# Attention with a routed mixture of experts: new places for the routing of the next-to-final batch, and two output copies on another engine

## The chip, the cores and the metric

The kernel runs on one core of a Trainium2 chip. A core has five engines that run side by side and wait for one another through semaphores: TensorE (PE, the matrix engine; PEld is its weight load), VectorE (DVE), ScalarE (ACT), GpSimd (POOL) and SyncE (SP), which here only starts transfers. The metric is the device time of one execution in microseconds (us). The kernel before takes 797.64 us, the median of three runs (795.63 to 798.19).

## The reference

There are two halves. The first is causal attention for 8 batches of 8 heads, 576 rows each, head size 64, with a bias from a running sum:

```
bias   = -(cum[:, :, :, None] - cum[:, :, None, :])
scores = where(causal, -1e9, q @ k.T / 8 + minimum(bias, 0))
attn   = softmax(scores);  x = attn @ v
```

The second takes the 4608 rows of `x` (512 wide) through one of 8 experts each:

```
logits = x @ w_gate;  e = argmax(logits);  gate = softmax(logits)[e]
out    = gate * (maximum(x @ w1[e], 0) @ w2[e])
```

## The kernel before, in words

**Attention.** Heads go in 32 pairs, four pairs to a batch of 576 rows. The class Attention walks a loop of turns; in turn n each engine gets what the table `ORDER` lists, item by item, each with an offset that says which pair the item is for (pair = n - offset). The order in which the program issues these items is the order of the instructions on PE, DVE, ACT and POOL, since the loop runs under a manual schedule. Items that matter here, for turn n:

- `S0` to `S4`: the score products of five row groups on PE, each into a buffer `s`, of which there are two, used in rotation (pool `ps_s`, PSUM); `R..`: masked row maximum on DVE, which frees that buffer; `X..`: exponential on ACT.
- `T0` to `T4`: transposes of the exponentials on PE into a buffer `t` (two of these as well, pool `ps_t`); `E0` and `E4` copy the result to `aT` on DVE, `E1` to `E3` on ACT (line 325 and 324, the function `copy`).
- `AV`: attention times v on PE (line 335), 36 matmul records for one pair, for the pair of the turn before; it too takes a buffer `t`. `XB`: its output goes to `xb` by the function `keep`, on DVE, one turn later still.

Turn 31 is the last with scores; turn 32 has the rest of pair 31, up to its AV.

**Routing.** When the four pairs of a batch are in `xb`, the batch is routed in eight steps, the generator `route`. Its first part issues PE work into an `s` buffer; after the `yield` comes the work of another engine that empties it. Step 0: logits (PE, line 378), then the copy `LT` on ACT. Step 1: transposes of `LT` (PE), then `part` on DVE, after which the generator lives on as `self.chain`, in three more pieces: sums to `dd` (DVE, four instructions, lines 400 to 409), `ex` (ACT, line 411), one-hot and gate (DVE, six small instructions, lines 413 to 423). Step 2: ranks by counting (PE), then the row numbers `dsi` (DVE, lines 439 to 445). Steps 3 to 7: transpose one fifth of the rows (PE), then scale it into `xr` (DVE, line 455). When `dsi` is there, each finished fifth of `xr` can be scattered to its expert's region of the DRAM tensor `xs` by an indirect transfer that POOL starts (line 464).

Batches 0 to 5 are routed in slots of the table: `rp` issues the PE part, `rv` or `ra` the other engine's part some items later. Batch 6, the next-to-final one, is routed in turns 29 to 32 by the list `HASTE`: at each `rp` item the function `hurry` issues whole steps, both parts of a step one straight behind the other, and a -1 or -2 stands for two pieces of the chain. Its scatters are issued at the items `SC` and `SD` and after the loop. Batch 7 is routed after the loop, between the matmuls of expert 0.

**Experts.** After the loop come, in program order, the load of the first 512 rows of expert 0 (`load_x`, line 657), which waits for every scatter issued so far, that is batches 0 to 6; the conversion of the first half of w1 into two rounded parts (`load_w`: ACT high part, line 648, POOL low part, line 649); transposes of the loaded rows (`trans_groups`, line 694), their split (ACT and DVE, lines 626 and 627), and layer 1 of expert 0 (line 722). Weight blocks (`raw`, 1 MB) have two buffers; the third load can go when POOL has converted the first. From there on an expert follows an expert.

The names `p0` to `p7` and `v0` to `v7` in the change are the PE part and the other engine's part of the steps 0 to 7, and `c` is one piece of the chain.

Of the kernel before, what the change touches and what calls it, by code (L numbers as in the profile page):

```python
# [20 lines left out]
B, H, S, D = 8, 8, 576, 64  # L21
# [19 lines left out]
RUNP = NPAIR  # L41
# [1 line left out]
SPLITS = {"QH": 0, "QL": 1, "KH": 2, "KL": 3, "QD": 4}  # L43
EVAC = {0: "V", 1: "A", 2: "A", 3: "A", 4: "V"}
STEPS = (3, 0), (1, 4), (5, 6), (2, 7)
HASTE = [0], [3, 1], [4, -1], [-2, 5], [2, 6], [7], [], []
NROUTE = 8
W_STEP = 2
THIN_AT = (2, 2)
# [23 lines left out]
class Attention:  # L73
# [97 lines left out]
    def load(self, p):  # L171
        x = self.ldx.tile([P, 2 * S], F32, name="qk")
        self.nc.sync.dma_start(x, self.qkv[p][:, : 2 * S])
        self.st.setdefault(p, {}).update(x=x)
# [166 lines left out]

    def keep(self, p):
        b, x = divmod(p, 4)
        self.copy("V", self.xb[b % 2][:, x, :S], self.st.pop(p)["O"])

    def fresh(self, b):
        nc = self.nc
# [128 lines left out]
    def loop(self):  # L476
        self.load(2)
        self.load_v(1)
        self.rows, self.sq, self.chain, self.slot = {}, [], None, {}
        self.haste, self.nrow = list(HASTE), {}  # L480
        self.todo = constants(self.nc, self.const, self.K, self.wg)
        for n in range(-3, RUNP + 3):
            for name, off in ORDER:
                if 0 <= n - off < RUNP:
                    self.item(name, n - off)
        while self.sq:
            self.scatter(*self.sq.pop(0))
        assert self.nfill > E
        self.open = False

    def item(self, name, p):
        kind, arg = name.rstrip("0123456789"), [int(x) for x in name if x.isdigit()]
        if kind == "S":
            if p < 2 and arg[0] == ORD[0]:
                self.load(p + 3)
                if p == 0:
                    self.load_v(2)
                    self.table(3)
            self.scores(p, arg[0])
            if p == 1:  # L500
                next(self.todo, None)
        elif kind == "R":
            self.rowmax(p, *arg)
            self.nrow[p] = self.nrow.get(p, 0) + 1
            if self.nrow[p] == 2 * NG - 1:
                for load, n in (self.table, 4), (self.load_v, 3), (self.load, 5):
                    if p + n < RUNP:
                        load(p + n)
        elif kind == "DM":
            self.causal(p)  # L510
        elif kind == "X":
            self.expo(p, *arg)
            if name == "X11" and 2 <= p and self.nfill <= E:
                for _ in range(2):
                    if self.nfill <= E:
                        self.fill(self.nfill)
                        self.nfill += 1
        elif kind == "T":
            self.st[p]["E", arg[0]] = self.trans(p, arg[0])
        elif kind == "E":  # L520
            self.st[p].pop(("E", arg[0]))()
        elif kind == "AV":
            self.av(p)
        elif kind == "XB":
            self.keep(p)
        elif kind in SPLITS:
            if p:
                self.split(p, SPLITS[kind])
        elif kind in ("SC", "SD"):
            if self.sq and (p >= RUNP - 4 or p % 4 < 2 + (kind == "SC")):  # L530
                self.scatter(*self.sq.pop(0))
        elif p >= 4 or kind in ("ch", "ca"):
            self.routing(kind, p, *arg)

    def routing(self, kind, p, k=0):
        b, x = p // 4 - 1, p % 4
        if kind == "ch" and x == 3:
            self.fresh(p // 4)
        if b == RUNP // 4 - 2:
            if kind == "rp":  # L540
                self.hurry(self.rows[b], self.haste.pop(0))
            elif kind == "ch" and x == 0 and "rr" not in self.rows[b]:
                self.scale(self.rows[b])
        elif kind == "rp":
            self.begin(p, k, self.rows[b], STEPS[x][k])
        elif kind in ("rv", "ra"):
            if (p, k) in self.slot and (kind == "ra") == (self.slot[p, k][1] == 0):
                self.end(p, k)
        elif kind == "ch" and x == 0 and b >= 0:
            self.scale(self.rows[b])  # L550
        elif self.chain and (x == 2 or kind == "ch" and x == 3):
            next(self.chain, None)

    def hurry(self, r, steps):
        if "rr" not in r:
            self.scale(r)
        for x in steps:
            if x < 0:
                for _ in range(2):
                    next(self.chain, None)  # L560
            else:
                self.begin(RUNP, 0, r, x)
                self.end(RUNP, 0)

    def begin(self, p, k, r, x):
        todo = self.route(r, x)
# [448 lines left out]
```

## Time and profile before

| what | value |
|---|---|
| median of three runs | 797.64 us |
| the profiled execution | 792.23 us |
| its span | 790.5 us |
| PE busy | 754.3 us, 95% of the span |
| DVE busy | 453.3 us, 57% |
| ACT busy | 416.8 us, 53% |
| POOL busy | 252.1 us, 32% |

The profiled execution is one run, 5.4 us under the median of the others; 1.7 us of it lies around the span. Sums of trace durations are made against its 792.23 us. PE is busy nearly throughout, so what counts is where PE waits. The page's slices show one dip of the clock that PE was granted in the middle of the span, in the slice from 316 to 336 us: it is the passage from attention to the experts.

### The profile page before, as it was taken

What the parts mean: (1) busy time and instruction counts of PE and PEld (TensorE: products, weight loads), DVE (VectorE), ACT (ScalarE), POOL (GpSimd) and SP (SyncE); (2) the same over time, 40 slices, a digit from 0 to 9 for tenths busy, and PEclk for the clock granted to TensorE, in tenths of its full rate; (3) what the DMA queues carried; (4) which work ended last, traced back from release to release, by engine and by line L of the source; (5) the groups of instructions that cost most, each with busy time, mean ns of one, the idle gap of its engine ahead of it and who ended that gap; (6) DMA issues with size and microseconds to landing.
All of it is one profiled execution on the core that took longest, in us unless ns stands there. A gap on an engine that the chain in (4) does not pass through costs nothing.

```text
span 790.5 us, 17552 instructions
## 1 busy us (share of the span) xinstructions
PE 754.3 (95%) x6664; PEld 583.3 (74%) x6664; DVE 453.3 (57%) x1234; ACT 416.8 (53%) x1001; POOL 252.1 (32%) x362
## 2 busy tenths in 40 slices
PE   7899999999999986799899999999999999999995
PEld 4667777777777764478788887888888887888874
DVE  5777988888898976454163453632632452633420
ACT  4998989999898975423152332412522341513410
POOL 5565677676767662221001001010000001010001
PEclk9999999999999999799999999999999999999998
DMA  7999776777767342459253452620530261720101
GB/s 256 323 320 290 221 249 204 229 226 218 239 220 232 125 152 88 162 178 335 87 196 129 162 174 83 203 89 29 189 134 27 92 231 46 240 95 21 53 29 40
DMA packets 57344, 130.80 MB, mean 165 GB/s; under 512 B 5455, under 2 KB 5455, under 8 KB 57232
## 3 DMA queue, kind: packets, MB, share of 16 engines
q1 hardware_dynamic: 48768, 105.53, 42.0%
q0 software_dynamic: 5936, 18.92, 6.3%
q10 hardware_dynamic: 2528, 4.89, 1.9%
q8 instruction: 67, 1.10, 0.6%
q14 instruction: 45, 0.37, 0.1%
HBM read 101.30 MB, written 28.27 MB: 164 GB/s over the span
## 4 chain that ended last, share of the span: by engine, by line
issue 38%; PE 7%; DMA 6%; another core or an unknown queue 4%; POOL 2%; POOLq 1%; ACT 0%; DVE 0%
DMA out_dram<-y,xr 6%; PE ph L722 3%; PE py L744 3%; POOL out_dram L751 2%; PE t L335 1%; PE t L694 0%; POOLq L844 0%; PE t L302 0%; PE t L378 0%; POOLq L751 0%; POOLq L1010 0%; ACT xT L626 0%; DVE y L750 0%; PE t L702 0%
## 5 line engine op out<-in xcount | busy, mean ns | idle before, releaser
L744 PE MATMUL py<-w2t,hT 128*128 128x512 f32 x768 | 181.4, 392 | 1.0 <-DVEq L858 1.0
L298 ACT ACTIVATE E<-z,m 128x512 f32<-128x512 f32 (+4 forms) x288 | 166.7, 583 | 28.4 <-DVE m L284 21.4
L722 PE MATMUL ph<-xT,w1t 128*128 128x512 f32 x768 | 178.2, 391 | 1.7 <-ACT xT L626 1.2
L722 PEld LDWEIGHTS ph<-xT,w1t 128*128 128x128 f32 x768 | 143.6, 188 | 33.6 <-issue 2.5
L744 PEld LDWEIGHTS py<-w2t,hT 128*128 128x128 f32 x768 | 142.5, 188 | 31.3 <-issue 1.4
L751 POOL DMA_INDIRECT out_dram<-y,xr x39 | 38.1, 977 | 397.3 <-DVE y L750 332.2
L284 DVE CUSTOM_DVE_ANT_0 z<-s,B 128x512 f32<-128x512 f32 (+3 forms) x224 | 116.0, 543 | 15.3 <-PE s L226 7.1
L335 PE MATMUL t<-aT,v 128*64 128x64 f32 (+4 forms) x1152 | 96.3, 322 | 1.3 <-ACT w1t L648 1.0
L226 PE MATMUL s<-kh,q 64*128 64x128 f32 (+3 forms) x512 | 93.1, 372 | 2.5 <-DVE m L284 1.3
L724 ACT ACTIVATE hT<-ph 128x512 fp32r<-128x512 f32 x64 | 38.2, 598 | 102.1 <-PE ph L722 97.1
L750 DVE TENSOR_SCALAR y<-py,xr 128x512 f32<-128x512 f32 x35 | 26.3, 750 | 114.5 <-PE py L744 114.5
L725 DVE SCALAR_TENSOR_TENSOR hT<-ph,hT 128x512 fp32r<-128x512 f32 x64 | 44.1, 690 | 67.4 <-ACT hT L724 63.8
L302 PE MATMUL t<-ident,E 64*128 64x64 f32 x1600 | 75.7, 227 | 6.9 <-ACT aT L325 3.1
L302 PEld LDWEIGHTS t<-ident,E 64*128 64x128 f32 x1600 | 63.8, 139 | 22.1 <-issue 9.6
L325 ACT COPY aT<-t 128x1024 f32<-128x1024 f32 (+2 forms) x96 | 73.1, 795 | 10.0 <-PE t L302 5.1
L226 PEld LDWEIGHTS s<-kh,q 64*128 64x128 f32 x512 | 52.1, 187 | 29.9 <-DVE aT L324 23.5
L335 PEld LDWEIGHTS t<-aT,v 128*64 128x64 f32 x1152 | 51.5, 139 | 22.2 <-issue 11.6
L298 ACT ACTIVATION_READ_ACCUMULATOR E<-z,m 128x1 f32 x288 | 55.4, 192 | 0.0
L464 POOL DMA_INDIRECT xs<-xr,dsi x40 | 40.1, 1001 | 41.5 <-DVE num L966 18.7
L626 ACT ACTIVATE xT<-t 128x512 fp32r<-128x512 f32 x32 | 17.6, 597 | 66.9 <-PE t L694 58.8
L207 POOL TENSOR_TENSOR kl<-qk,kh 128x576 fp32r<-128x576 f32 x30 | 42.6, 1422 | 29.4 <-ACT kh L203 29.4
L324 DVE COPY aT<-t 128x256 f32<-128x256 f32 x64 | 39.6, 619 | 12.6 <-PE t L302 8.6
(157 smaller groups left out, 970.7 us busy)
## 6 DMA issues: line engine op xcount, KB each, us to landing
raw<-in_w_dram SPq DMA_DIRECT2D x32, 1024.0 KB
qk<-in_qkv_dram SPq DMA_DIRECT2D x32, 576.0 KB
B<-cum SPq DMA_DIRECT2D x31, 512.0 KB
v<-in_qkv_dram SPq DMA_DIRECT2D x32, 320.0 KB
B<-cum SPq DMA_DIRECT2D x62, 144.0 KB
xr<-xs SPq DMA_DIRECT2D x8, 1028.0 KB
xs<-blank ACTq DMA_DIRECT2D x9, 514.0 KB
xs<-blank SPq DMA_DIRECT2D x8, 514.0 KB
```

The costliest lines, as they stand in the source:

```text
L207: e.tensor_tensor(out=d["kl"], in0=k, in1=d["kh"].bitcast(F32), op=ALU.subtract)
L226: self.nc.tensor.matmul(out, terms[n][0], terms[n][1], start=begin and n == 0, stop=n == len(terms) - 1, skip_group_check=True)
L284: ins = nc.vector.tensor_tensor_reduce(out=cut(z[:, :w]), in0=x, in1=mask, scale=-0.125, scalar=3.0e38, op0=ALU.add, op1=ALU.min, accum_out=m,
L298: nc.scalar.activation(out, z[:, :w], AF.Exp, bias=m, scale=-1.0, accum_out=total)
L302: self.nc.tensor.transpose(out, src[r], self.K["ident"][r, r])
L325: return self.nc.scalar.copy(o, i)
L335: nc.tensor.matmul(ps[64 * h : 64 * h + 64, bank, lo - 512 * bank : hi - 512 * bank], v[:, kt, h], self.aT[p % 2][:, kt, h, lo:hi], start= ...
L464: ins = self.nc.gpsimd.indirect_dma_start(out=self.K["xs"], out_offset=IndirectOffsetOnAxis(ap=r["dsi"][:n, k : k + 1], axis=0), in_=r["xr ...
L722: nc.tensor.matmul(ps, w[:, a, d, c], x[:, b, d], start=n == 0, stop=n == 11)
L725: nc.vector.scalar_tensor_tensor(out=h[:, 1, f], in0=ps, scalar=0.0, in1=h[:, 0, f].bitcast(F32), op0=ALU.max, op1=ALU.subtract)
L744: self.nc.tensor.matmul(ps, hT[:, a, f, c], w[:, b, f % 4], start=f == 0 and i == 0, stop=f == 7 and i == 2)
L751: disjoint(self.tc, "out", self.nc.gpsimd.indirect_dma_start(out=self.out, out_offset=IndirectOffsetOnAxis(ap=row[:, DM + 1 : DM + 2].bitc ...
```

## The change

The list `HASTE` becomes a table: behind the item on the left, of the pair after the colon, stands the part on the right. Each part of each step of batch 6 has a place of its own, so the PE part and the part that empties its buffer are no longer issued one straight behind the other. All steps stand in turns 29 to 31; before, the last one stood in turn 32. In `hurry`, as soon as `dsi` exists, every fifth that is ready is scattered at once. And `keep` copies the outputs of pairs 30 and 31 on ACT.

```diff
-HASTE = [0], [3, 1], [4, -1], [-2, 5], [2, 6], [7], [], []
+HASTE = {
+    "T4:28": "p0", "ra1:27": "v0", "rp0:28": "p1", "rv0:28": "v1", "ch:29": "c", "SC:29": "c",
+    "XB:28": "c", "rp1:28": "p3", "rv1:28": "v3", "rp0:29": "p2", "rv0:29": "v2", "E0:30": "p4",
+    "XB:29": "v4", "rp1:29": "p5", "rv1:29": "v5", "rp0:30": "p6", "rv0:30": "v6", "T1:31": "p7", "ch:31": "v7",
+}
...
-        self.copy("V", self.xb[b % 2][:, x, :S], self.st.pop(p)["O"])
+        self.copy("V" if p < RUNP - 2 else "A", self.xb[b % 2][:, x, :S], self.st.pop(p)["O"])
...
+        for x in HASTE.get(f"{name}:{p}", "").split():
+            self.hurry(self.rows[RUNP // 4 - 2], x)
...
-            if kind == "rp":
-                self.hurry(self.rows[b], self.haste.pop(0))
-            elif kind == "ch" and x == 0 and "rr" not in self.rows[b]:
+            if kind == "ch" and x == 0:
                 self.scale(self.rows[b])
...
-    def hurry(self, r, steps):
-        if "rr" not in r:
-            self.scale(r)
-        for x in steps:
-            if x < 0:
-                for _ in range(2):
-                    next(self.chain, None)
-            else:
-                self.begin(RUNP, 0, r, x)
-                self.end(RUNP, 0)
+    def hurry(self, r, x):
+        if x[0] == "c":
+            next(self.chain, None)
+        elif x[0] == "p":
+            self.begin(RUNP, int(x[1]), r, int(x[1]))
+        else:
+            self.end(RUNP, int(x[1]))
+            while r["b"] == RUNP // 4 - 2 and "dsi" in r and self.sq:
+                self.scatter(*self.sq.pop(0))
```

How it moves instructions, in three places. The first is ACT in turn 30 of the kernel before, from the last exponential of `E_104` for its second row group to the copies `E3` and `E1` of pair 30; `ex` is the chain's piece of batch 6.

```order
L298 ACTIVATE E_102,sums_208<-z,m 128x128
L298 ACTIVATE E_104,sums_208<-z,m 128x384
L411 ACTIVATE ex<-dd 128x40
L325 COPY aT_107<-t 128x2x8x64
L325 COPY aT_107<-t 128x2x4x64
L298 ACTIVATE E_104,sums_208<-z,m 128x384
```

In the changed kernel `ex` stands a turn earlier, in turn 29, behind the two copies of pair 29 (to the other `aT`) and behind the second `E_104`; the piece begins with the copy `LT` of step 0:

```order
L329 COPY LT<-s 128x576
L329 COPY aT_107<-t 128x2x6x64
L302 ACTIVATE E_102,sums_208<-z,m 128x128
L302 ACTIVATE E_104,sums_208<-z,m 128x384
L329 COPY aT_108<-t 128x2x8x64
L329 COPY aT_108<-t 128x2x4x64
L302 ACTIVATE E_104,sums_208<-z,m 128x384
L415 ACTIVATE ex<-dd 128x40
```

So nothing but exponentials stands ahead of the two copies in turn 30 now.

The second place is the end of attention on ACT in the kernel before: the copy `E2` of pair 31, then the first half of w1 and the split of expert 0's rows.

```order
L298 ACTIVATE E_106,sumx_209<-z,m 128x576
L325 COPY aT_108<-t 128x2x6x64
L648 ACTIVATE w1t<-raw 128x512 x4
L626 ACTIVATE xT<-t 128x8x64 x4
L626 ACTIVATE w1t<-raw 128x512 x4
```

And in the changed kernel, with the two output copies (`xb`, pairs 30 and 31):

```order
L302 ACTIVATE E_106,sumx_209<-z,m 128x576
L329 COPY xb_206<-t 128x576
L329 COPY aT_108<-t 128x2x6x64
L329 COPY xb_206<-t 128x576
L651 ACTIVATE w1t<-raw 128x512 x4
L629 ACTIVATE xT<-t 128x8x64 x4
L629 ACTIVATE w1t<-raw 128x512 x4
```

The second copy, which needs the AV of pair 31, stands ahead of the w1 conversion and of the split.

The third place is POOL from the last bias table to the w1 conversion, in the kernel before: two scatters of batch 5, row numbers for batch 7, five scatters of batch 6.

```order
L169 TENSOR_TENSOR B<-B,mixed 128x64
L464 DMA xs<-xr,dsi 38912x514 x2
L350 IOTA xr 128x5
L464 DMA xs<-xr,dsi 38912x514 x5
L649 TENSOR_TENSOR w1t<-raw,w1t 128x512 x4
```

In the changed kernel four of the five have moved ahead of the row numbers:

```order
L173 TENSOR_TENSOR B<-B,mixed 128x64
L468 DMA xs<-xr,dsi 38912x514 x6
L354 IOTA xr 128x5
L468 DMA xs<-xr,dsi 38912x514
L652 TENSOR_TENSOR w1t<-raw,w1t 128x512 x4
```

Each scatter follows the DVE part that fills its rows, and these are in turns 30 and 31 now.

## Rows read from the trace of the kernel before

**Rows 1.** Timeline: start, duration, engine, line, operation, count, [idle before <- releaser]; AV by pair.

```profile
267.28 2.96 PE L335 MATMUL t<-aT,v 128*64 128x64 f32 x36
276.06 2.96 PE L335 MATMUL t<-aT,v 128*64 128x64 f32 x36
286.79 2.96 PE L335 MATMUL t<-aT,v 128*64 128x64 f32 x36
299.67 2.96 PE L335 MATMUL t<-aT,v 128*64 128x64 f32 x36
309.57 2.96 PE L335 MATMUL t<-aT,v 128*64 128x64 f32 x36 [0.36 <-ACT aT L325]
317.34 4.62 PE L335 MATMUL t<-aT,v 128*64 128x64 f32 x36 [0.97 <-ACT w1t L648]
```

**Rows 2.** Timeline of turn 30, where PE, DVE and ACT wait for one another.

```profile
291.28 0.53 PE L302 MATMUL s<-ident,LT 64*128 64x64 f32 x10 [0.79 <-DVE xr L455]
...
291.85 0.55 DVE L392 TENSOR_TENSOR part<-s,ra 128x160 f32<-128x160 f32 x2 [0.63 <-PE s L302]
...
297.81 0.24 ACT L411 ACTIVATE ex<-dd 128x40 f32<-128x40 f32 x1 [2.27 <-DVE dd L409]
297.95 1.48 ACT L325 COPY aT<-t 128x1024 f32<-128x1024 f32 x2
...
299.00 0.34 PE L302 MATMUL t<-ident,E 64*128 64x64 f32 x4 [1.95 <-ACT aT L325]
```

**Rows 3.** Timeline of turn 31, the same view.

```profile
302.68 0.76 DVE L324 COPY xb<-t 128x576 f32<-128x576 f32 x1 [1.06 <-PE t L335]
...
305.17 0.44 PE L226 MATMUL s<-kh,q 64*128 64x384 f32 x2 [1.06 <-DVE xr L455]
...
307.81 1.71 ACT L325 COPY aT<-t 128x1024 f32<-128x1024 f32 x2 [0.21 <-PE t L302]
```

**Rows 4.** Timeline of turn 32 and of the passage to expert 0.

```profile
314.94 0.76 DVE L324 COPY xb<-t 128x576 f32<-128x576 f32 x1 [2.98 <-remote]
315.16 0.80 ACT L325 COPY aT<-t 128x768 f32<-128x768 f32 x1 [4.28 <-remote]
...
315.86 2.19 ACT L648 ACTIVATE w1t<-raw 128x512 fp32r<-128x512 f32 x4
316.41 0.83 DVE L324 COPY aT<-t 128x640 f32<-128x640 f32 x1
316.57 0.92 POOL L464 DMA_INDIRECT xs<-xr,dsi  x1 [2.45 <-PE t L302]
...
317.50 4.95 POOL L649 TENSOR_TENSOR w1t<-raw,w1t 128x512 fp32r<-128x512 f32 x4
319.51 0.37 SPq L657 DMA_DIRECT2D xr<-xs  x1
...
324.75 1.97 PE L694 MATMUL t<-ident,xr 64*128 64x64 f32 x32 [2.79 <-issue]
325.95 0.60 ACT L626 ACTIVATE xT<-t 128x512 fp32r<-128x512 f32 x1 [7.90 <-issue]
...
327.96 1.22 PE L722 MATMUL ph<-xT,w1t 128*128 128x512 f32 x2 [1.24 <-ACT xT L626]
...
335.33 1.14 ACT L626 ACTIVATE w2t<-raw 128x512 fp32r<-128x512 f32 x2
```

**Rows 5.** Timeline of ACT: a copy of an output's size.

```profile
284.51 0.64 ACT L325 COPY LT<-s 128x576 f32<-128x576 f32 x1 [1.12 <-PE s L378]
```

**Rows 6.** Windows: stretch, its length, PE busy, granted clock, DMA share, GB/s.

```profile
318.00:322.00 4.00, 3.96 (x26) 0.61 0.46 104
...
328.00:331.00 3.00, 3.00 (x18) 0.50 0.00 0
350.00:360.00 10.00, 10.00 (x46) 1.00 0.84 262
```

**Rows 7.** One line's instructions: all scatters to xs, min/median/max in ns.

```profile
L464 POOL DMA_INDIRECT xs<-xr,dsi x40: 917/994/1440, 92.4 to 346.8; - x40
```

More of the change, by code (lines that the diff above doesn't have):

```diff
@@ L479, in loop @@
         self.rows, self.sq, self.chain, self.slot = {}, [], None, {}
-        self.haste, self.nrow = list(HASTE), {}
+        self.nrow = {}
         self.todo = constants(self.nc, self.const, self.K, self.wg)
```

## The prediction

> **What bounds the kernel now.** PE is busy nearly all the time, so I looked for the stretches in which it is not: first the slices of the page, which show one dip of PE's granted clock between the halves, then a timeline of that stretch, then windows for the clock. The expert half is plain: from 350 to 360 us PE is busy all of the time at full clock [rows 6], and what moves the start of layer 1 of expert 0, the matmul at 327.96 [rows 4], moves the end with it.
>
> Between the halves the AVs of the pairs are a good ruler [rows 1]. From pair 26 to 27 they are 8.78 us apart, a turn that PE fills. The turns with the routing of batch 6 are longer: 10.73, then 12.88, then 9.90, though that third one has two score groups less to compute. The last AV begins 7.77 us after the one before, and takes 4.62 us instead of 2.96.
>
> In turn 30 PE waits 0.79 us for a buffer that DVE has yet to empty, and 1.95 us for a copy on ACT; ACT was late because `ex` stood ahead of the two copies and waited 2.27 us for DVE's `dd` [rows 2]. In turn 31 PE waits 1.06 us for the scaling of one fifth of the rows, which held a score buffer [rows 3]. In turn 32 all is late by one event: DVE's copy of pair 30's output starts at 314.94, though the AV that it reads ended at 309.57 + 2.96 = 312.53, and ACT's next copy starts at 315.16; both have a releaser that the profile can't name [rows 1, 4]. The last fifth of the rows is then scattered at 316.57, the load that waits for all scatters goes at 319.51, its rows are transposed from 324.75, and layer 1 starts at 327.96 [rows 4]. The last AV ended at 321.96, so 6.0 us lie between.
>
> **The change part by part.** The instructions are the same ones; two copies change engine. What counts is who waits.
>
> Turn 29. PE gets the ten transposes of step 1 (0.53 us, [rows 2]) a turn earlier and step 0 earlier within the turn, and DVE the chain's first pieces. Both have room: the turn was 1.95 us over the plain 8.78. It may lose the 0.53 or win as much by waits that vanish; I take 0, and keep 0.5 on both sides.
>
> Turn 30. `ex` leaves the head of ACT's queue there (front: first place), so the 1.95 goes. Steps 3 and 1 no longer share a slot, so the 0.79 goes: 2.74 together. In their place PE has the short matmuls of step 2, and DVE six small instructions of the chain ahead of the row maxima, which I put at 1.2 us (none should be longer than one of the two `part`, 0.28), against the 0.55 of `part` and its 0.63 of wait that leave [rows 2]. I take 2.4 of the 2.74; the ends are 1.0 and 2.74.
>
> Turn 31. Step 4 now holds a score buffer over the end of the turn, until DVE has copied an output (0.76, [rows 3]) and scaled a fifth of the rows (put at 0.7). Step 5 needs that buffer, so PE waits about 1 us early in the turn, where it waited 1.06 later [rows 3]. Whatever PE does, the next AV waited for ACT's two copies (307.81 + 1.71 = 309.52, AV at 309.57, [rows 1, 3]). I take 0, with 1 us on both sides.
>
> Turn 32. Without the stall after 312.53 the path is: output copy on ACT, 0.64 as the copy of the same size in [rows 5], ten transposes, DVE's copy of 0.83 [rows 4], then the AV: about 2.4 us, counted from 314.94 to 317.34. In place of the 4.81 us from 312.53 to 317.34, this is a gain of 2.4. Whether the stall goes is the largest unknown, since its cause isn't shown: the ends are 0 and 2.4. Nothing in the program but that AV holds the copy back, and the copy of the pair before started 0.05 us after its AV's end (299.67 + 2.96 = 302.63, the copy at 302.68, [rows 1, 3]). By this nearest row I take 2.4.
>
> The last AV. It took 1.66 us more than the others, while the granted clock stood at 0.61 of full in the mean of 318 to 322, so for most of that at its lower level, 1.2 GHz [rows 1, 6]. Before that fall PE had done little for the 4.8 us since the AV of pair 30. With 2.4 us there instead I expect the AV to be over before a fall: 1.66, the ends 0 and 1.66.
>
> From the last AV to layer 1. The load no longer ends this. The last scaling stands in turn 31 ahead of the AV of pair 30, at 309.57 - 2.4 = 307.2 in the new time; a scatter takes 0.92, the load went 2.94 us after its last scatter's start (316.57 to 319.51) and its rows were in use 5.24 us later [rows 4]: 307.2 + 2.94 + 5.24 = 315.4. The last AV would begin at 307.2 + 2.96 + 2.4 = 312.5 and end at 315.5. So they arrive together. But ACT's queue now has the second output copy ahead of the w1 conversion (front: second place), which before was long done by then: 0.64, then 2.19 for the four conversions, then from the first split of the rows to layer 1 the 2.01 of before (325.95 to 327.96): 4.84 us after the AV [rows 4, 5]. Against 6.0 this is still 1.15 better, though 2.83 of the 4.84 is a wait that the change puts there.
>
> The clock behind it. From 328 to 331 PE is at the lower level throughout, so the first 3.0 us of layer 1 ran at half speed [rows 6], a loss of 1.5. In the new order PE idles some 3 us ahead of layer 1, so the fall comes later, and more of the slow stretch may lie on layer 1: between 0 and 1.5 more lost, the second if the slow part there doubles. I take 1.0.
>
> Scatters beside work. They now start while DVE and POOL are at work. All 40 scatters of the kernel take 917 to 1440 ns, median 994, and most of these stand in the loop beside DVE work [rows 7]; so I leave their time as it is. The Trainium skill's page "SBUF — State Buffer", section "SBUF: two separate sides", speaks against this move: GpSimd writes the descriptors of its transfers through a port that DVE can lock, and a transfer of some 620 ns took some 3100 ns beside a DVE copy. The trace doesn't show it for these scatters. By that rule the last scatter would be some 2.1 us longer, an estimate from row and page; the rows would come at 317.5, and layer 1 some 0.6 us later, so the sum would be 6.0.
>
> Sum: 2.4 + 2.4 + 1.66 + 1.15 - 1.0 = 6.6 us gained. The profiled execution would take 792.2 - 6.6 = 785.6; the median of the runs, 5.4 above it, 797.6 - 6.6 = 791.0. About 0.3%, 2.4 us, is what a measurement can tell from no change.
>
> **The rivals.**
> 1. The stall of turn 32 is bound to something that stays (the end of the loop, not the scatters), and the clock falls on the last AV again. For it: the releaser is unknown. Against: no other output copy waits so. Gain 2.4 + 1.15 - 0 = 3.6, time 794.0.
> 2. The waits are only shifted. The second output copy holds back POOL's w1 low parts too, which need ACT's high parts and take 4.95 [rows 4], and with them the first buffer that the third weight block needs. Before, that was free at 322.45; now at about 315.5 + 0.64 + 0.55 + 4.95 = 321.6, hardly earlier, while layer 1 starts 6.6 us earlier. Its first use came 7.4 us after layer 1 began (335.33, [rows 4]), so now at about 328.7, and the block needs some 5 us like the load of the rows: 326.6. That fits by 2 us. With other transfers in the way ACT stands before the split of layer 1's outputs, and PE stops by 2 to 5 us; time 793 to 796.
> 3. Slower. With steps kept open, one of two score buffers is held from p to v in each of turns 29 to 31, so scores stop at eight places for DVE's part. A price is the 1.06 of [rows 3]; eight of these are 8.5 us, and more than six of them eat the gain. From there, 797.6 - 6.6 + 8.5 = 799.5. Against it: the batches before use such slots, and the turn of 8.78 had two steps of batch 5 in it.
> 4. It doesn't do what it says, as the next thing behind the AVs (ACT's exponentials) was the bound of turn 30 all along: no gain there, and the rest as in rival 1, so 1.2; time 796.4.
>
> **How the numbers follow.** My forecast, 791.0, with its neighbours (gain 4.5 to 10): 55 in 100. Rival 1: 20. Rival 2: 10. Rival 4: 8. Rival 3: 7. Adding the unknown ends upward (turns 29 and 31 by 1.5, no loss by the clock 1.0, turn 30 by 0.3) gives a gain of 9.4, time 788.2, so the low end is 788.0. The high end takes in rivals 1 and 2 whole: 796.3. Faster by over 0.3%: the forecast, rival 1 but for 4, and half of rival 2, 55 + 16 + 5 = 76. Within 0.3%: these 4 and 5, and rival 4, 17. Slower by over 0.3%: rival 3, 7, though it needs nearly all of its waits for that.
>
> **What would show it.** AV of pair 29 some 10.5 us after that of pair 28, not 12.9; no wait of ACT before `ex` in turn 30; AV of pair 31 about 5.4 us after that of pair 30 and 2.96 long; the load of the rows sent before 312; layer 1 starting 4.8 us after the last AV's end, with ACT's w1 conversion as what it waited for. The forecast fails if the stall with no named releaser comes again, if PE has waits for score buffers of 1 us in several places of turns 29 to 31, or if layer 1 has a gap at its second output for want of a weight block.

## The result and the profile after

The changed kernel takes 786.69 us (median of four runs, 782.78 to 789.46) against 797.91 us (795.63 to 798.81) for the kernel before: ratio 0.9875, interval 0.985 to 0.9899. That is 11.2 us less. Forecast were 6.6 less, 791.0, in 788.0 to 796.3: the direction was right, the time lies below the range. The profiled executions differ by less: 792.23 to 786.29, that is 5.9 us, at the same mean clock of 0.986. Half of this document is about that difference of differences. One of the seven runs of e_step7late, below, took 1835.44 us; it stands in no ratio, and the median given is that of the other six.

The AVs of the changed kernel and the first matmuls behind them, from the timeline of PE (start, duration, ...), answering to [rows 1, 4]; in the fences of this document other instructions between the lines are left out, also where no dots stand:

```profile
277.00 2.96 PE L339 MATMUL t<-aT,v 128*64 128x64 f32 x36
287.02 2.96 PE L339 MATMUL t<-aT,v 128*64 128x64 f32 x36
297.37 2.96 PE L339 MATMUL t<-aT,v 128*64 128x64 f32 x36
308.36 2.96 PE L339 MATMUL t<-aT,v 128*64 128x64 f32 x36
313.55 2.96 PE L339 MATMUL t<-aT,v 128*64 128x64 f32 x36 [0.97 <-ACT aT L329]
317.76 1.21 PE L697 MATMUL t<-ident,xr 64*128 64x64 f32 x32 [1.25 <-issue]
321.16 1.22 PE L725 MATMUL ph<-xT,w1t 128*128 128x512 f32 x2 [2.19 <-ACT xT L629]
...
327.51 4.64 PE L725 MATMUL ph<-xT,w1t 128*128 128x512 f32 x19
332.67 1.19 PE L725 MATMUL ph<-xT,w1t 128*128 128x512 f32 x4
```

Turn 30 shrank from 12.88 to 297.37 - 287.02 = 10.35 us, and the last AV is 2.96 us long. Layer 1 starts 12.80 us after the AV of pair 30, where it took 18.39 before [rows 1, 4]. But turn 31 grew, from 9.90 to 10.99. Other engines, in the timeline of all of them, show why, and what holds layer 1 now:

```profile
287.34 0.24 ACT L415 ACTIVATE ex<-dd 128x40 f32<-128x40 f32 x1
...
303.29 0.98 POOL L468 DMA_INDIRECT xs<-xr,dsi  x1 [0.30 <-DVE xr L459]
...
304.88 0.82 DVE L328 COPY aT<-t 128x640 f32<-128x640 f32 x1 [1.90 <-PE s L230]
...
309.59 0.93 POOL L468 DMA_INDIRECT xs<-xr,dsi  x1 [0.17 <-issue]
...
312.54 0.37 SPq L660 DMA_DIRECT2D xr<-xs  x1
...
316.54 0.64 ACT L329 COPY xb<-t 128x576 f32<-128x576 f32 x1 [3.84 <-PE t L339]
317.08 2.19 ACT L651 ACTIVATE w1t<-raw 128x512 fp32r<-128x512 f32 x4
```

`ex` no longer waits. The last scatter starts 6.98 us earlier than in [rows 4]. In turn 31 a copy on DVE starts at 304.88, though the last transposes that it reads (22 from 302.09, for 0.85 us) were done at 302.94: a late start beside scatters (302.01 and 303.29), like the one that left turn 32; it comes 0.61 us after the second scatter has ended. In another trace of this kernel, below, the same copy starts 0.04 us behind them. And layer 1 waits for ACT, which does the output copy and the w1 conversion (316.54 to 319.27) ahead of the row splits, as step "last AV to layer 1" had it: 4.65 us behind the last AV's end, forecast 4.84.

### The profile page after: what moved, and what is told of

It is laid out like the page before. It is cut to its first block, busy times and chain, and to the rows that moved or that the text cites. A ratio compares the mean times of both kernels' runs of the same rounds, so it can differ in the third digit from the quotient of the medians.

```text
span 784.6 us, 17552 instructions
## 1 busy us (share of the span) xinstructions
PE 753.0 (96%) x6664; PEld 583.4 (74%) x6664; DVE 452.2 (58%) x1232; ACT 418.0 (53%) x1003; POOL 251.4 (32%) x362
## 4 chain that ended last, share of the span: by engine, by line
issue 40%; PE 37%; DMA 9%; POOL 4%; another core or an unknown queue 4%; DVE 3%; ACT 2%; POOLq 1%; ACTq 0%; DVEq 0%
PE s L230 11%; PE t L339 10%; DMA out_dram<-y,xr 6%; PE t L306 6%; PE ph L725 3%; PE py L747 3%; POOL out_dram L754 2%; DMA qk<-in_qkv_dram 2%; DVE z L288 1%; PE s L306 1%; DMA v<-in_qkv_dram 1%; PE s L382 1%; ACT aT L329 1%; POOL kl L211 1%
## 5 line engine op out<-in xcount | busy, mean ns | idle before, releaser
L339 PE MATMUL t<-aT,v 128*64 128x64 f32 (+4 forms) x1152 | 94.6, 318 | 1.1 <-ACT aT L329 1.0
L328 DVE COPY aT<-t 128x256 f32<-128x256 f32 x64 | 39.6, 619 | 16.1 <-PE t L306 11.2
```

Source lines behind the costliest of these rows:

```text
L339: nc.tensor.matmul(ps[64 * h : 64 * h + 64, bank, lo - 512 * bank : hi - 512 * bank], v[:, kt, h], self.aT[p % 2][:, kt, h, lo:hi], start= ...
```

## The experiments

They ran on four further chips, each timed against the kernel before on its own chip; starts in two traces are compared as distances only. The first chip is that of the result; the second ran c_before, c_after, e_xbA and e_xbV, the third e_step7late, e_step7early and the two e_warm, the fourth e_ex, e_scatlate, e_mix and r_xbV, the fifth b_ctl and b_late.

**The same two kernels again.** No edit.

c_before: 

> The kernel before once more, to learn which of its executions the first trace was (792.2 us, though its timed runs were 795.6 to 798.8). Theory A (the clock): the timed gain of 10 us is larger than the 6.8 us that layer 1 starts earlier in the two traces because a typical execution of the kernel before has PE at the lower clock for longer than its first trace shows: times 795 to 799, a mean granted clock of 0.979 to 0.983 instead of 0.986, and a trace with some 8 to 15 us more at half clock than the 20.5 us of the first one (up to 7 us of time). Theory B (the waits): a typical execution waits longer between attention and experts, by a stall without a named releaser like the one at 312.5: same clock, 0.986, layer 1 of expert 0 starting at 331 or later instead of 328.

c_after: 

> The changed kernel once more, on the same chip as the others here. Both theories: about 0.987 of the kernel before (786 to 788), turn 31 about 11 us long, layer 1 starting 4.6 us after the last AV's end. Theory A: the times among its runs fall as their mean granted clock rises, by about 0.7 us for 0.001. Theory B: no such order in its runs.

Measured: c_before 790.77, ratio 0.9997 (0.9978 to 1.0016); c_after 781.31, ratio 0.9882 (0.986 to 0.9903). So the effect holds, and here the two profiled executions (791.06 and 780.93) differ by about as much as the medians. The theories of c_before did not come as put: its mean clock, 0.982, is that of A, but the time lies under A's, and B's stall is absent. From the timelines of PE and POOL, c_before:

```profile
284.01 2.96 PE L335 MATMUL t<-aT,v 128*64 128x64 f32 x36
296.42 4.62 PE L335 MATMUL t<-aT,v 128*64 128x64 f32 x36
307.99 2.96 PE L335 MATMUL t<-aT,v 128*64 128x64 f32 x36 [0.36 <-ACT aT L325]
312.82 0.92 POOL L464 DMA_INDIRECT xs<-xr,dsi  x1 [0.30 <-issue]
313.38 2.96 PE L335 MATMUL t<-aT,v 128*64 128x64 f32 x36 [0.96 <-ACT w1t L648]
...
323.09 1.97 PE L694 MATMUL t<-ident,xr 64*128 64x64 f32 x32 [6.75 <-issue]
326.30 1.22 PE L722 MATMUL ph<-xT,w1t 128*128 128x512 f32 x2 [1.24 <-ACT xT L626]
...
337.54 1.21 PE L722 MATMUL ph<-xT,w1t 128*128 128x512 f32 x4
```

and c_after:

```profile
284.35 2.96 PE L339 MATMUL t<-aT,v 128*64 128x64 f32 x36
294.36 2.96 PE L339 MATMUL t<-aT,v 128*64 128x64 f32 x36
303.90 2.96 PE L339 MATMUL t<-aT,v 128*64 128x64 f32 x36
304.88 0.94 POOL L468 DMA_INDIRECT xs<-xr,dsi  x1 [0.17 <-DVE rr L364]
309.09 2.96 PE L339 MATMUL t<-aT,v 128*64 128x64 f32 x36 [0.97 <-ACT aT L329]
...
316.70 0.74 PE L725 MATMUL ph<-xT,w1t 128*128 128x512 f32 x2 [2.42 <-ACT xT L629]
...
327.62 1.20 PE L725 MATMUL ph<-xT,w1t 128*128 128x512 f32 x4
```

This kernel before has no stall in turn 32 (the last AVs are 5.39 us apart, not 7.77) and no slow last AV. Instead the AV of pair 29 is the slow one, 4.62 us, and PE then waits 6.75 us for the rows. Turn 31 of c_after takes 9.54 us, not the 11 expected: the late start of the first chip is absent. By stages, in us (from AV to AV, then to layer 1 and to its group of four matmuls):

| stage | forecast gain | first pair | second chip |
|---|---|---|---|
| turn 29 | 0 | 10.73 to 10.02: 0.71 | 10.30 to 10.00: 0.30 |
| turn 30 | 2.4 | 12.88 to 10.35: 2.53 | 12.41 to 10.01: 2.40 |
| turn 31 | 0 | 9.90 to 10.99: -1.09 | 11.57 to 9.54: 2.03 |
| AV of pair 30 to layer 1 | 5.2 | 18.39 to 12.80: 5.59 | 18.31 to 12.80: 5.51 |
| layer 1 to its group of four | -1.0 | 10.74 to 11.51: -0.77 | 11.24 to 10.92: 0.32 |
| sum | 6.6 | 6.97 | 10.56 |

At the AV of pair 27 the changed trace is 0.94 and 0.64 us behind (277.00 against 276.06, 274.35 against 273.71). 6.97 - 0.94 = 6.03 stands against 5.94 in the whole, 10.56 - 0.64 = 9.92 against 10.13: the stretch holds nearly all of it.

**The copies on ScalarE.** e_xbA is the kernel before with the diff's `keep` line alone. e_xbV and r_xbV are the changed kernel without it, e_mix has pair 30 on ScalarE alone:

```
e_xbA:         self.copy("V" if p < RUNP - 2 else "A", ...)      # in before
e_xbV, r_xbV:  self.copy("V", ...)                               # in after
e_mix:         self.copy("A" if p == RUNP - 2 else "V", ...)     # in after
```

e_xbA: 

> The kernel before with only the two output copies on ScalarE. There the w1 conversion had 7.9 us of room before the rows came, so it gets 2.8 us later and just fits: layer 1 starts at the same time after the rows, and the time is that of the kernel before within 0.5 us. If the copies matter in themselves: 1 us faster. If the queue matters already there: up to 1 us slower.

e_xbV: 

> The changed kernel with the output copies of pairs 30 and 31 on VectorE again. The w1 conversion on ScalarE no longer stands behind the last copy. If that queue alone set the start of layer 1, it starts 2.8 us earlier after the last AV's end (1.8 instead of 4.65): 784 us. If the load of the rows (transposed 1.25 us after the AV's end) sets it next, it starts about 2.4 to 3.2 us after the rows come, so 1 us earlier: 785.7. Rival: the copies on ScalarE were themselves a gain (0.1 us each by duration, and VectorE's queue is free for the copy E4): then slower than the changed kernel by up to 1 us.

e_mix: 

> The changed kernel with only the output copy of pair 30 on ScalarE and that of pair 31 on VectorE again. Theory (the copy on ScalarE ahead of the w1 conversion is what layer 1 waits for, the other copy is the path to the last AV and costs the same on either engine): layer 1 starts 11.4 to 12.0 us after the AV of pair 30 begins instead of 12.8, and the time is 0.5 to 1.5 us under the changed kernel's, so about that of both copies on VectorE; ratio to before 0.985 to 0.989. Rival (the load behind the last scatter sets layer 1 anyway): 12.4 to 12.8 us, and the ratio of the changed kernel, 0.9875 to 0.9885.

r_xbV: 

> The changed kernel with both output copies on VectorE, again, on another chip beside the other two: ratio to before 0.985 to 0.989 as in its first runs (0.9869); the AV of pair 30 to layer 1 in 11.7 to 12.2 us. If the first result was chance of that trace, 12.8 us.

Measured: e_xbA 1.0007 (0.9992 to 1.0021), e_xbV 0.9869 (0.9845 to 0.9893), e_mix 0.9873 (0.984 to 0.9906), r_xbV 0.9871 (0.9839 to 0.9903). Alone the two copies do nothing. In the new order the one of pair 31 costs: layer 1 starts 11.86, 11.99 and 12.10 us after the AV of pair 30 in e_xbV, e_mix and r_xbV, against 12.80. From the timelines of e_mix:

```profile
304.26 2.96 PE L339 MATMUL t<-aT,v 128*64 128x64 f32 x36
...
308.49 2.20 ACT L651 ACTIVATE w1t<-raw 128x512 fp32r<-128x512 f32 x4
309.45 2.96 PE L339 MATMUL t<-aT,v 128*64 128x64 f32 x36 [0.97 <-ACT w1t L651]
...
316.25 0.73 PE L725 MATMUL ph<-xT,w1t 128*128 128x512 f32 x2 [1.59 <-ACT xT L629]
```

ACT's w1 conversion is over at 310.69, before the last AV ends at 312.41. Then the rows themselves (their transposes start 1.05 us behind the AV) and DVE's splits are next in line. The 0.8 us can't be told from none in the medians, and no version is shown to beat the changed kernel.

**Turn 30 alone.** e_ex is the kernel before, but the chain's second piece stands behind ACT's two copies:

```
-                for _ in range(2):
+                for _ in range(-x):
                     next(self.chain, None)
...
+            if name == "SC" and p == RUNP - 2:
+                next(self.chain)
```

> The kernel before with one instruction moved: the exponential `ex` of the routing stands on ACT behind turn 30's two copies, just ahead of the AV, instead of ahead of them; nothing else changes. Theory (PE's 1.95 us wait for the copy in turn 30 comes from `ex` at the head of ACT, and that wait is what lets the clock fall on the AV of pair 29): turn 30 becomes 1.3 to 2.0 us shorter, the AV of pair 29 takes 2.96 us instead of the 4.4 to 4.6 it mostly has, and the time falls by 1.5 to 3.5 us, ratio 0.9955 to 0.998. Rival (the wait only moves to the slots that steps 3, 1 and 4 share, or ACT's exponentials are the bound): turn 30 less than 0.7 us shorter, ratio within 0.9985 to 1.0015. The stretch from the AV of pair 30 to layer 1 is untouched by either: about 18.4 us.

Measured: 789.67 us, ratio 0.9967 (0.9946 to 0.9989), so 2.6 us less. From the timeline, e_ex:

```profile
286.17 2.96 PE L335 MATMUL t<-aT,v 128*64 128x64 f32 x36
...
290.66 0.52 PE L302 MATMUL s<-ident,LT 64*128 64x64 f32 x10 [0.79 <-DVE xr L455]
...
296.46 2.96 PE L335 MATMUL t<-aT,v 128*64 128x64 f32 x36
296.73 0.24 ACT L411 ACTIVATE ex<-dd 128x40 f32<-128x40 f32 x1
...
306.36 2.96 PE L335 MATMUL t<-aT,v 128*64 128x64 f32 x36 [0.36 <-ACT aT L325]
```

Turn 30 takes 10.29 us by the move of one instruction, and the wait of 0.79 for the score buffer is still there. On this chip the old order took 12.42 (e_scatlate) and the new one takes 10.01 (e_mix), so `ex` alone is worth 2.13 of the 2.41, and the 0.79 at most the 0.28 that are left: I had added it to the 1.95 and taken something off again. The AV of pair 29 is 2.96 us long, and turn 31 9.90.

**Is it PE's wait that slows the AV of pair 29?** e_warm30 puts four extra matmuls into that wait of turn 30, e_warm32 fourteen behind the last AV (their results are not used):

```
+    def warm(self, ps, n):
+        for _ in range(n):
+            self.nc.tensor.matmul(ps[:HP], self.LT[:, :HP], self.LT[:, HP : HP + 512], ...)
```

e_warm30: 

> The kernel before with four extra matmuls (1.7 us of PE, results never used) in turn 30, where PE waits 1.9 us for ScalarE's copies. Theory A (clock): the AV of pair 29, which ran at half clock in two of three traces with the old routing, stays at full clock, turn 31 is 9.9 instead of 11.4 us, and the median falls by about 1 us (0.9985). Rival: the fall comes from something else than that wait (the waits before it, or chance): AV of pair 29 is slow as often, and the time is the same or up to 0.3 us more by matmuls that outlast the wait.

e_warm32: 

> The kernel before with fourteen extra matmuls (6 us of PE, results never used) behind the last AV, where PE waits 6.8 us for the rows of expert 0. Nothing that waits is taken away. Theory A (clock): PE doesn't fall to the lower clock there, or for 3 to 7 us less, layer 1 runs faster behind it, and the time falls by 2 to 4 us (0.995 to 0.9975). Theory B (waits alone): no change, or up to 1 us slower where the matmuls outlast the wait.

Measured: 1.001 (0.9987 to 1.0034) and 1.0128 (1.0084 to 1.0171). From the timeline of PE, e_warm30:

```profile
298.57 3.65 PE L368 MATMUL s<-LT 128*64 128x512 f32 x8
302.82 2.96 PE L335 MATMUL t<-aT,v 128*64 128x64 f32 x36
```

The AV is at full clock (granted 1.00 from 302.8 to 305.8); the same AV took 4.41, 4.62, 4.63, 5.48, 4.60, 3.83 and 3.87 us in e_xbA, c_before, e_step7early, e_warm32, e_scatlate, b_ctl and b_late, which have the old wait, and 2.96 in e_ex and in every kernel with the new order. In c_before the granted clock was 0.61 from 296.5 to 300.9. Only the first trace has the wait, 1.95, without the fall [rows 1, 2]. So the fall follows the wait, in seven of eight traces. But the eight passes took 3.65 us where 1.9 were free, which cost about what the AV won, and the median didn't fall as expected. e_warm32 overshot by far: its passes took 12.18 us, so the time says nothing. But PE was busy up to the rows at a granted clock of 1.00, and from layer 1's start to its group of 19 matmuls it then took 4.20 us, against 6.60 in e_warm30 on the same chip: the slow clock at the start of layer 1 costs some 2.4 us there.

How much of the path the clock still takes is in the windows (stretch, length, PE busy, granted clock, DMA share, GB/s; the number of matmul records in brackets), c_before:

```profile
270.00:310.00 40.00, 35.14 (x510) 0.96 0.29 100
310.00:340.00 30.00, 20.86 (x197) 0.83 0.40 137
```

e_ex, in the first of the two:

```profile
270.00:310.00 40.00, 37.04 (x578) 1.00 0.33 114
```

c_after, in the second:

```profile
310.00:340.00 30.00, 26.48 (x198) 0.94 0.56 185
```

and e_mix, in the second:

```profile
310.00:340.00 30.00, 27.27 (x214) 1.00 0.63 212
```

`ex` gives back the first stretch. The earlier rows give back the second, in which PE had idled with the load: with the last fifth late again (e_step7late, next) it is 0.83 there as in c_before.

**The last fifth of the rows.** e_step7late is the changed kernel with step 7 back in turn 32; e_step7early is the kernel before with step 7 in turn 31:

```
-... "rv0:30": "v6", "T1:31": "p7", "ch:31": "v7",
+... "rv0:30": "v6", "rp1:30": "p7 v7",
-HASTE = [0], [3, 1], [4, -1], [-2, 5], [2, 6], [7], [], []
+HASTE = [0], [3, 1], [4, -1], [-2, 5], [2, 6, 7], [], [], []
```

e_step7late: 

> The changed kernel with step 7 (the last fifth of batch 6) back in turn 32, both parts straight behind one another, as before. Theory A' (two separate gains: the load chain behind the last fifth, and PE's waits with the clock in turns 30 and 31): the last scatter is again after the output copy of pair 30, the load lands late, from the AV of pair 30 to layer 1 it is 18 us again instead of 12.8, and the kernel loses 4.5 to 5.5 us, to about 0.995 of the kernel before. Rival (the load isn't what PE waits for; the passage got shorter since all of turns 29 to 31 did): within 1 us of the changed kernel, 0.988.

e_step7early: 

> The kernel before with only step 7 moved up, behind steps 2 and 6 in the last rp slot of turn 31, both parts still together. Theory A': the load chain's share alone, the way from the AV of pair 30 to layer 1 down from 18.3 to about 13 to 14 us, the turns before unchanged, time 0.994 of before. Rival (all from turns 30 and 31): within 0.2% of before. Second rival: step 7 holds a buffer and DVE in turn 31, that turn grows by 1 to 2 us and eats part of it: 0.996.

Measured: 791.86 us, 0.9937 (0.9912 to 0.9962); 794.43 us, 0.9967 (0.9947 to 0.9986). From the timeline, e_step7late:

```profile
310.13 2.96 PE L339 MATMUL t<-aT,v 128*64 128x64 f32 x36
...
314.49 0.93 POOL L468 DMA_INDIRECT xs<-xr,dsi  x1 [3.29 <-PE t L306]
...
322.59 1.97 PE L697 MATMUL t<-ident,xr 64*128 64x64 f32 x32 [4.31 <-issue]
325.80 1.22 PE L725 MATMUL ph<-xT,w1t 128*128 128x512 f32 x2 [1.24 <-ACT xT L629]
```

With the last scatter in turn 32, PE waits 4.31 us for the rows again, and the AV of pair 30 is 15.67 us from layer 1 instead of 12.80; 18 were expected, but turn 32 has no stall in this order. The ratio lies 0.0055 to 0.0062 above the changed kernel's, on other chips. In the old order step 7 early gives 15.14 us instead of 18.4, but its turn 31 takes 13.21 us, against 11.57 in c_before, so half of that is gone, as the second rival had it. So the place of step 7 is worth most when the others have moved too.

**Do the scatters bring the late start in turn 32?** In e_scatlate the five scatters were to stand behind POOL's low parts of the first weight block, by the order of the code; b_late does that by a dependency, and b_ctl is the kernel before beside it:

```
-            if self.sq and (p >= RUNP - 4 or ...):
+            if self.sq and p < RUNP - 2 and (p >= RUNP - 4 or ...):
...                                                   # flushed behind load_w(1, 0, 0)
+            after(self.tc, ins, [self.K["w1lo"]])    # b_late alone: wait for the low parts
```

e_scatlate: 

> The kernel before with the five scatters of the next-to-final batch held back on POOL until the low parts of the first weight block are done there (about 322 us), so that POOL issues no transfer while turn 32 runs. Theory A (the late start of DVE's output copy before turn 32, 2 to 2.4 us in some traces, comes from POOL issuing scatters one behind another): the copy of pair 30's output starts within 0.2 us of its AV's end, and the AV of pair 31 begins 5.2 to 5.5 us after that of pair 30. Theory B (it comes from something else at the end of the loop): the copy is 2 us late as before, 7.7 us between the AVs, if the kernels beside it on this chip show that. In both the rows come late: last scatter at about 328, load 331, layer 1 at 337 to 340, so the whole time is 7 to 12 us above the kernel before, ratio 1.009 to 1.015.

b_ctl: 

> The kernel before, unchanged, as the measure for b_late on this chip. Either DVE's copy of pair 30's output starts about 2.4 us after its AV's end (7.7 us between the last two AVs), as in the first trace, or within 0.7 us (5.4 us between them), as on two other chips; five scatters about 1.3 us apart lie around it. In the second case this pair can't tell the theories apart.

b_late: 

> The kernel before with the five scatters of the next-to-final batch behind POOL's low parts of the first weight block, by a dependency. Theory A (POOL's scatters bring the late start): the copy of pair 30's output starts within 0.7 us of its AV's end and the last two AVs begin 5.2 to 5.5 us apart, also where b_ctl shows 7.7. Theory B (something else at the end of the loop): 7.7 here too where b_ctl shows it. In both: POOL's low parts begin at about 314 to 317, the first scatter 5 us later, the last 5.2 us after it, the load 3 to 4.5 us behind that, layer 1 about 7.5 us after the load; so layer 1 starts 4 to 7 us later than in b_ctl, and the time is 4 to 8 us longer.

Measured: e_scatlate 1.0005 (0.9985 to 1.0025). Its scatters ran at 308.53 to 313.73, ahead of the low parts at 314.66, as without the edit: it tested nothing, and is one more trace of the kernel before without the stall (5.39 us between the last AVs, layer 1 18.23 us behind the first of them). b_ctl 799.82 and b_late 807.07 us, one run each. From the timeline of b_ctl:

```profile
314.24 2.96 PE L335 MATMUL t<-aT,v 128*64 128x64 f32 x36 [0.36 <-ACT aT L325]
...
317.80 0.98 POOL L464 DMA_INDIRECT xs<-xr,dsi  x1 [0.30 <-issue]
319.66 0.76 DVE L324 COPY xb<-t 128x576 f32<-128x576 f32 x1 [3.04 <-remote]
...
322.06 4.62 PE L335 MATMUL t<-aT,v 128*64 128x64 f32 x36 [0.96 <-ACT w1t L648]
...
334.67 1.22 PE L722 MATMUL ph<-xT,w1t 128*128 128x512 f32 x2 [1.24 <-ACT xT L626]
```

and of b_late:

```profile
313.80 2.96 PE L335 MATMUL t<-aT,v 128*64 128x64 f32 x36 [0.36 <-ACT aT L325]
316.80 0.76 DVE L324 COPY xb<-t 128x576 f32<-128x576 f32 x1 [0.87 <-PE t L335]
...
319.19 2.96 PE L335 MATMUL t<-aT,v 128*64 128x64 f32 x36 [0.96 <-ACT w1t L648]
...
324.22 1.01 POOL L464 DMA_INDIRECT xs<-xr,dsi  x1 [0.28 <-POOL w1t L649]
```

Without scatters in turn 32 the copy starts 0.04 us after its AV's end, where it started 2.46 late with them, on the same chip; the last AVs are 5.39 instead of 7.82 us apart, and the last one runs at full clock. So theory A holds, by one trace each. The other traces fit it. Wherever the late start shows, DVE starts 0.6 to 1.3 us after the end of the last scatter of a run (b_ctl: 318.78 and 319.66; in the first trace the run of four ended at 314.11, and the copy starts at 314.94 [rows 4]). In the old order the copy is 2.41 to 2.51 us late in all five traces that have these scatters on the first, third and fifth chip. Layer 1 starts 7.8 us later than in b_ctl, a little more than the 4 to 7 expected, and the time is 7.3 longer, within the 4 to 8. On the second and fourth chip the copy starts 0.04 us behind its AV in the midst of the same scatters (c_before: five, started from 307.63 to 312.82; the copy at 310.99). Why, and by what way a scatter holds up DVE, stays open.

## Why the prediction was wrong

**The step that failed: "the median of the runs, 5.4 above it, 797.6 - 6.6 = 791.0".** By its own trace the sum was good: 6.6 forecast, 6.97 measured by stages, 5.9 in the whole; in part that is luck, since the errors of the stages (+0.7, +0.1, -1.1, +0.4, +0.2) cancel. But I carried over the 5.4 us between the profiled execution of before and its median as if it were a constant. It was not: the changed kernel's median is 0.4 above its profiled run, and c_before's median 0.3 under its own. Some of those 5.4, by my reading, were losses that this change removes, and which the one trace happened not to show. The term that comes of it is turn 31, forecast at 0 because AV and copies there stood at their plain times [rows 1, 3]. In seven other traces of the old wait the AV of pair 29 is slow by 0.9 to 2.5 us; on the second chip turn 31 gave 2.03. I had the cause in hand: I tied the last AV's slowness to PE's idleness ahead of it, and did not ask whether the waits of turn 30, which I listed, could do the same to the next AV in another execution. The unprofiled runs of the first pair left no trace; b_ctl, at 799.82 us, is the nearest to them. It is longer than [rows 1, 4] by 0.5 in turn 30, 0.9 in turn 31 (its AV takes 3.83), 2.0 from the AV of pair 30 to layer 1 and 0.6 behind it up to the long group of matmuls: 4.1 of 7.6 us. That is near the 5.3 by which the medians differ more than the two traces, but that the first chip's unprofiled runs lost the same is not shown. Another 3.2 of the 7.6 lie ahead of the AV of pair 27 (279.30 against 276.06), where the change moves nothing.

**Turn 29, 0: 0.3 to 0.7.** Within half a microsecond or little over it.

**Turn 30, 2.4: 2.4 and 2.5.** Right in size, and its cause is `ex` for 2.1 of it (e_ex), not the 0.79.

**Turn 32's stall, 2.4.** That the scatters behind one another on POOL bring it is shown (b_late), not the end of the loop as rival 1 had it. It did leave turn 32. But I overlooked that the scatters go along: in the first pair and on the third chip a late start of 1.9 stands beside them in turn 31 (304.88 above; 306.65 in e_step7late), 0.6 us behind their end; no run takes the scatters out of that place. So part was only moved, and the -1.09 of turn 31 in the first pair is of that order. Where a chip has no such stall, there was nothing to win by this term.

**The last AV, 1.66, and "last AV to layer 1", 1.15.** With the stall's 2.4 they sum to 5.2, and 5.5 to 5.6 were measured. On the second chip, though, the first two terms are nothing and the third is all: 9.96 us from the last AV's end (313.38 + 2.96) to layer 1 became 4.65. There the load bounds the passage. It does in the first trace too: PE waits 2.79 us for the rows behind the slow AV [rows 4], more than the 1.66, so that term alone would have won nothing. The three terms are one sum: from the AV of pair 30 to the last scatter, and from there to layer 1. Before, it was 7.00 + 11.39 us on the first chip, with the stall in the first part, and 4.83 + 13.48 on the second, without it; after, 1.23 + 11.57 and 0.98 + 11.82. So the place of step 7 is what wins (e_step7late: 4.36 + 11.31). What the stall costs the passage isn't shown: without it the way behind the scatter is 2.1 longer on the second chip, but b_ctl has the stall and the longer way, 7.05 + 13.38.

**The clock behind it, -1.0.** Measured -0.77 in the first pair and +0.32 on the second chip. The mean granted clock of the runs went from 0.983 to 0.987 there, so over the whole the clock was a gain on that chip. This may be the other part of the miss: the runs before on the first chip have no clock on record.

**Scatters beside work.** They kept their time on POOL: 907 to 1417 ns, median 992, against [rows 7]. The rule of the Trainium skill's page "SBUF — State Buffer" that I weighed (section "SBUF: two separate sides"), by which a transfer went from some 620 to some 3100 ns beside a DVE copy, isn't seen in these times. My price for it was 0.6 us at layer 1; by the same rows it is 0.4 (317.5 + 3.21 against 315.5 + 4.84). It is the other side that can suffer: b_ctl's DVE and ACT start late beside them (ACT's copy at 319.88).

**The rivals.** 1 is refuted above. 2: ACT's order does cost 0.8 us at layer 1's start (e_mix), but the third weight block was in time: the group of 19 matmuls and that of four begin 5.16 us apart in the changed trace (327.51 and 332.67), and in the one before as well. (In my working of this rival layer 1 starts 6.6 us earlier; by the terms ahead of layer 1 that is 7.6.) 3: PE does wait for score buffers, once in turn 30 (1.00 us at 292.45) and twice in turn 31 (0.73 at 301.79, 1.47 at 306.80, behind the late start), not eight times. 4 is refuted by e_ex.

## What to carry to other kernels

When the profiled run is faster than the median, ask what the slower runs lose and whether the change touches it, before carrying the gap over as a constant; runs of the kernel before on one further chip would have shown the slow AV. A wait of a microsecond or two on PE is priced with what may follow it: in seven of eight traces here the AV behind it ran in part at half clock and took 0.9 to 2.5 us more. And terms that stand in one row behind one deadline (a stall, a slow AV, a wait for the load) are one term: take the way to the last producer and from it to the consumer, and look at which of them is hidden behind it.

## What the runs showed of the hardware

- DVE and ACT can start some 2 us after what they wait for has ended, while POOL issues indirect transfers one behind another: 2.46 us in b_ctl, gone in b_late. Three of the five chips show it, two don't, with the same instructions; on the three the kernel before takes 797.9, 797.9 (medians) and 796.9 and 799.8 us (two single runs), on the two 791.4 and 792.5 (medians). The profile gives it a releaser of "remote" or a PE row long done.
- On one chip, the fourth, 23 executions of the kernel before took 787.89 us (mean granted clock 0.985) to 795.37 (0.978); the highest clock, 0.988, went with 789.27 and the lowest, 0.976, with 794.59 to 794.97.
- An extra f32 matmul (128*64 128x512) shows as two passes of 0.43 to 0.46 us each at a granted clock of 1.00 (12.18 us for 28, 3.65 for 8).
